# Twelve output-weight blocks instead of eight ahead of the last V tile, and their products behind it

## The chip, the core and the metric

The kernel runs on one core of one Trainium2 chip. The metric is the device time of one execution in microseconds (us). The kernel before was run three times: 680.56, 680.35 and 680.41 us, median 680.41. One further execution was profiled; every row of the trace quoted here is from that execution.

## What is computed

One decode step of grouped-query attention over a cache, gated by a small MLP. All data are float32.

```python
# x (8, 512); k_cache, v_cache (8, 8, 4096, 128); wq (512, 4096); wo (4096, 512)
xn = layernorm(x)
q  = heads(xn @ wq)                         # 8 batches, 32 heads of 128, 4 per cache head
p  = softmax(q . k_cache * 128 ** -0.5)     # over 4096 cached keys
o  = p . v_cache                            # (8, 32 heads, 128)
s  = o.reshape(8, 4096) @ wo                # (8, 512)
g  = silu(mlp(xn))                          # gelu, layernorm, scale, output projection
out = x + s * g
```

The caches are 268 MB of the 291 MB that are read, so the kernel is a stream of large loads with the arithmetic laid beside it.

## The kernel before

**Stages.** wq and the MLP's weights are loaded, q is projected and the MLP's gate worked out (L347 to L349). Then the loop of L350 goes over eight cache heads h. Each head takes two K tiles (`scores`, L269), a `softmax` (L272 to L298), and two V tiles (`values`, L310), one per half of the eight batches. A tile is 128 partitions x 64 KB, 8 MB, and goes into one of three buffers named `slot` (L67, L75). A load can start when the instructions that read the buffer's tile of three loads ago are done.

**Values and combine.** `values` multiplies one group of batches by V into one of two accumulators `o_ps`; VectorE then picks the diagonal (L313) and sums it (L315) into `o_sb`; `combine` (L320) folds `o_sb` into `po` by one small matmul, which is called one group late, so that TensorE has the next group to do meanwhile. The last V tile of the last head is loaded as two halves of 4 MB and is handled as two groups (n = 2); each group is 16 matmuls, and each shows as two records in the trace, 32 a group.

**Output weights.** wo is 32 blocks m of 128 x 512, 256 KB each; block m belongs to head m // 4 of the cache and its query row r = m % 4. All 32 share one slot buffer, loaded on the same queue (SyncE, SP) as everything else. The kernel before loads blocks 0 to 7 (`WO_EARLY = 8`, L359), then the last V tile's two halves (L332), then blocks 8 to 31 in nine pieces (`WO_PIECES`, L362) of 6, 5, 4, 3, 2, 1, 1, 1 and 1 blocks. Every load on the queue takes one of eight completion semaphores in turn, so it is not issued until the load eight before it has landed.

**Products of wo.** `project_o` (L344) multiplies blocks 0 to 27, whose heads are done early, into `part`, the first half of `sc`; the blocks r = 0 to 3 of a head go to four different 32-column strips of TensorE's array. Blocks 26 and 27 are cut in two halves of 256 columns each, to all four strips. `part` is then copied to SBUF (L383) and folded into the accumulator `acc` (L399). Blocks 28 to 31 belong to the last head; `direct` multiplies them straight into `acc` (L391) once `combine` has delivered that head: 28 and 29 ahead of L399, 30 and 31 behind it. VectorE multiplies `acc` by the gate, adds x (L403, L404), and the result is stored (L405).

**Order.** Each engine does its instructions in the order of its queue; a scheduler (Tile) makes the queues from the program's order and the dependences. In the kernel before, TensorE's queue around the end is: 32 matmuls of the first V tile of the last head; products 0 to 7; combine; 16 matmuls of the last tile's first half; combine; 16 matmuls of its second half; products 8 to 12; combine; products 13 to 27; direct 28, 29; L399; direct 30, 31.

Of the kernel before, what the change touches and what calls it, by code (L numbers as in the profile page):

```python
# [15 lines left out]
HKV, REP, S, DH = 8, 4, 4096, 128  # L16
NK = D // P
G = 4
J = S // (G * P)
R = 32  # L20
# [9 lines left out]
HALF = B // 2  # L30
# [1 line left out]
SLOT = HALF * UNIT  # L32
W = 64
OUT_ROWS = 2 * B
WO_EARLY = 8
WO_PIECES = [(8, 14), (14, 19), (19, 23), (23, 26), (26, 28), (28, 29), (29, 30), (30, 31), (31, 32)]
FOLDED = HKV * REP - REP
AHEAD = FOLDED + 2

# [20 lines left out]
def tile_gqa_gmlp_decode(ctx: ExitStack, tc: tile.TileContext, x, kT, v, wq, wo, w_mlp, w_ex0, w_ex1, w_ex2, w_ex3, out, gate, stored):  # L60
    nc = tc.nc
# [12 lines left out]
    def slot():  # L74
        return ring.tile([P, SLOT], F32, name="slot")  # L75
# [188 lines left out]
    def scores(h, half, k_sb):  # L264
        for i in range(HALF):
            b = half * HALF + i
            for c in range(2):
                for g in range(G):
                    nc.tensor.matmul(sc[R * g:R * (g + 1), c, :], qz[:, h, b * R:(b + 1) * R],  # L269
                                     k_sb[:, i, c, g, :], start=(b == 0), stop=(b == B - 1))  # L270

    def softmax(h):  # L272
        m = nm[:, h:h + 1]
        nc.vector.tensor_reduce(m, sc, op=ALU.max, axis=AX.XY, negate=True)  # L274
        p = work.tile([P, J * P], F32, name="p")
        nc.scalar.activation(p, sc.rearrange("p c s -> p (c s)"), AF.Exp,  # L276
                             bias=m, accum_out=l[:, h:h + 1])
        a = scratch([1, P], "a")
        nc.tensor.transpose(a, m, ident)  # L279
        nmin = small.tile([1, R], F32, name="nmin")  # L280
        nc.vector.tensor_reduce(nmin, a.rearrange("b (g r) -> b r g", g=G), op=ALU.min, axis=AX.X)
        full = small.tile([1, G, R], F32, name="full")
        nc.vector.tensor_copy(full, nmin[:, None, :].to_broadcast([1, G, R]))  # L283
        mm = scratch([P, 1], "mm")
        nc.tensor.transpose(mm, full.rearrange("b g r -> b (g r)"), ident[:1, :1])  # L285
        w = small.tile([P, 1], F32, name="w")
        nc.vector.tensor_sub(w, mm, m)
        nc.scalar.activation(w, w, AF.Exp)
        wl = small.tile([P, 1], F32, name="wl")
        nc.vector.tensor_mul(wl, w, l[:, h:h + 1])  # L290
        tot = scratch([P, 1], "tot")
        nc.tensor.matmul(tot, same_all, wl, start=True, stop=True)  # L292
        nc.vector.reciprocal(wl, tot)
        nc.vector.tensor_scalar(p, p, w, wl, op0=ALU.mult, op1=ALU.mult)  # L294
        pT = work.tile([P, J, B, G, REP], F32, name="pT")
        nc.vector.transpose(pT.rearrange("p j b g r -> p j g b r"),  # L296
                            p.rearrange("p (j g b r) -> p j g b r", j=J, g=G, b=B))
        return pT.rearrange("p j b g r -> p j b (g r)")  # L298
# [3 lines left out]
    def values(b0, n, pT, v_sb):  # L302
        o = o_ps[turn[0] % 2]
        turn[0] += 1
        of = o.rearrange("p g d -> p (g d)")
        rows = HALF // n
        for j in range(J):
            for i in range(n):
                c = i * rows + j % rows
                nc.tensor.matmul(of[R * c:R * c + G * REP, :], pT[:, j, b0 + i],  # L310
                                 v_sb[:, i, j], start=(j < rows), stop=(j >= J - rows))
        o_all = work.tile([P, G, DH], F32, name="o_all")
        nc.vector.tensor_mul(o_all, o, diag[:, :, None].to_broadcast([P, G, DH]))  # L313
        o_sb = small.tile([P, DH], F32, name="o_sb")
        nc.vector.tensor_reduce(o_sb, o_all.rearrange("p g d -> p d g"), op=ALU.add, axis=AX.X)  # L315
        return b0, n, o_sb

    def combine(b0, n, o_sb, po):
        f = fold if n == HALF else fold_last
        nc.tensor.matmul(po[:, b0 * REP:(b0 + n) * REP], o_sb, f.rearrange("p i r -> p (i r)"),  # L320
                         start=True, stop=True)

    def load_k(h, half):
        t = slot()
        nc.sync.dma_start(t, kT[h, half])
        return t.rearrange("p (i c g s) -> p i c g s", i=HALF, c=2, g=G)

    def load_v(h, half, parts):
        t = slot()
        n = SLOT // parts  # L330
        for c in range(parts):
            nc.sync.dma_start(t[:, c * n:(c + 1) * n], v[h, half][:, c * n:(c + 1) * n])  # L332
        return t.rearrange("p (i j e) -> p i j e", i=HALF, j=J)
# [3 lines left out]
    def project_o(lo, hi):  # L337
        for m in range(lo, hi):
            h, r = divmod(m, REP)
            cuts = 2 if m >= FOLDED - 2 else 1  # L340
            n = D // cuts
            for i in range(cuts):
                q = 2 * (r % 2) + i if cuts == 2 else r
                nc.tensor.matmul(part[R * q:R * q + B, i * n:(i + 1) * n], oT[:, h, r, :],  # L344
                                 wo_sb[:, m, i * n:(i + 1) * n], start=(m < REP), stop=(cuts == 2))
# [4 lines left out]
    for h in range(HKV):  # L350
        for half in range(2):
            scores(h, half, load_k(h, half))
        pT = softmax(h)
        po = po_ps[:, h % 2]
        for half in range(2):
            last = h == HKV - 1 and half == 1
            if last:
                wo_slot = slot()
                nc.sync.dma_start(wo_slot[:, :WO_EARLY * D], wo[:, :WO_EARLY * D])  # L359
                v_sb = load_v(h, half, 2)  # L360
                for lo, hi in WO_PIECES:
                    nc.sync.dma_start(wo_slot[:, lo * D:hi * D], wo[:, lo * D:hi * D])  # L362
                wo_sb = wo_slot.rearrange("p (m d) -> p m d", d=D)
                project_o(0, WO_EARLY)
            else:
                v_sb = load_v(h, half, 1)
            n = 2 if last else HALF
            for i in range(0, HALF, n):
                done = values(half * HALF + i, n, pT, v_sb[:, i:i + n])
                if half or i:  # L370
                    combine(*o_prev, po)
                o_prev = done
        combine(*o_prev, po)
        po_t = po.rearrange("p (b r) -> p r b", r=REP)
        if h < HKV - 1:
            nc.vector.tensor_copy(oT[:, h], po_t)
        else:
            for a in range(2):
                nc.vector.tensor_copy(oT_last[:, :, a, a * B:(a + 1) * B], po_t)

    project_o(WO_EARLY, FOLDED)
    part_sb = work.tile([P, G, DH], F32, name="o_all")
# [13 lines left out]
    for a in range(2):  # L396
        for g in range(G):
            c = (2 * g + a) * W
# [56 lines left out]
```

## Time and profile before

| | |
|---|---|
| median of three runs | 680.41 us (680.35 to 680.56) |
| the profiled execution | 680.28 us, of which the trace's span is 678.8 us |
| TensorE (PE) busy | 344.0 us, 51% of the span |
| VectorE (DVE) busy | 83.4 us, 12% |
| DMA | 290.80 MB read from HBM, 428 GB/s over the span |
| chain of work that ended last | DMA 79%, PE 16%, issue 4% |

Times in a view are us from the span's start. PE rows are matmuls, PEld rows weight loads, SPq rows the moments at which SyncE issues a transfer; the number behind the "x" is a count of records, and what stands in brackets is the idle time ahead of the first one and what ended it. A float32 matmul of 128 x 512 leaves two records. Matmuls are pipelined, so the time from the start of one to the start of the next tells what it costs, and the duration of one record is longer than that. A clock of 1.00 in a window is TensorE at full speed, 0.50 at half.

### The profile page before, as it was taken

The page shows a single profiled execution, that of the slowest core. Times are in us where ns is not written, and L with a number is a line of the kernel's source. Part 1 is how long each engine was busy: PE and PEld are TensorE (multiplying, and loading weights), DVE is VectorE, ACT ScalarE, POOL GpSimd, SP SyncE. Part 2 cuts the span into 40 slices and gives each one's busy share as a digit, 9 for nine tenths or more (in the row PEclk, how much of TensorE's full clock was granted, in tenths as well). Part 3 has the DMA queues.
Part 4 walks back from the last instruction along what each step waited for, and adds up shares of the span by engine and source line. Part 5 has one row for each costly group of instructions (what it writes and reads, how often), then busy time and mean ns, then how long its engine had stood idle before and what let it go on. Part 6 is the DMA issues. An engine that isn't in the chain of part 4 may idle for free.

```text
span 678.8 us, 5218 instructions
## 1 busy us (share of the span) xinstructions
PE 344.0 (51%) x2415; PEld 92.5 (14%) x2415; DVE 83.4 (12%) x159; ACT 13.4 (2%) x27; POOL 7.9 (1%) x17
## 2 busy tenths in 40 slices
PE   0448744446655454555554344555544345555567
PEld 0112211111111011111111011111111011111111
DVE  1143021102110021101100021101101021100221
ACT  0010000000000000000000000000000000000000
POOL 3000000000000000000000000000000000000000
PEclk9987866787776568777666778877666787876679
DMA  9999999999999999999999999999999999999997
GB/s 386 453 441 430 430 433 430 433 430 433 434 433 430 433 433 430 433 441 440 434 433 430 436 436 434 440 434 433 430 433 430 433 433 434 430 436 433 419 427 315
DMA packets 6741, 291.16 MB, mean 429 GB/s; under 512 B 888, under 2 KB 888, under 8 KB 1688
## 3 DMA queue, kind: packets, MB, share of 16 engines
q1 hardware_dynamic: 6576, 290.80, 99.1%
q8 instruction: 19, 0.31, 0.2%
q10 hardware_dynamic: 144, 0.03, 0.0%
q14 instruction: 2, 0.02, 0.0%
HBM read 290.80 MB, written 0.03 MB: 428 GB/s over the span
## 4 chain that ended last, share of the span: by engine, by line
DMA 79%; PE 16%; issue 4%; DVE 0%; SPq 0%; POOLq 0%; POOL 0%
DMA slot<-in_kT 36%; DMA slot<-in_v 33%; PE sc L269 7%; PE o_ps L310 7%; DMA slot<-in_wo 7%; DMA slot<-in_x 3%; PE scr L224 1%; PE scr L228 1%; SPq L332 0%; PE scr L217 0%; DVE st L146 0%; POOLq L449 0%; POOL rstd L149 0%; PE scr L206 0%; PE acc L391 0%
## 5 line engine op out<-in xcount | busy, mean ns | idle before, releaser
L269 PE MATMUL sc<-slot,qz 128*32 128x512 f32 x1024 | 145.4, 731 | 131.2 <-DMA slot<-in_kT 131.2
L310 PE MATMUL o_ps<-slot,pT 128*16 128x512 f32 x1024 | 148.2, 743 | 110.0 <-DMA slot<-in_v 110.0
L269 PEld LDWEIGHTS sc<-slot,qz 128*32 128x32 f32 x1024 | 38.1, 131 | 232.0 <-issue 149.4
L310 PEld LDWEIGHTS o_ps<-slot,pT 128*16 128x16 f32 x1024 | 32.9, 114 | 211.0 <-issue 151.5
L274 DVE TENSOR_REDUCE nm<-sc 128x1 f32<-128x1024 f32 x8 | 9.8, 1225 | 273.7 <-PE sc L269 273.7
L313 DVE TENSOR_TENSOR o_all<-o_ps,diag 128x512 f32<-128x512 f32 x17 | 11.8, 692 | 244.8 <-PE o_ps L310 244.8
L276 ACT ACTIVATE p<-sc,nm 128x1024 f32<-128x1024 f32 x8 | 8.9, 1114 | 551.8 <-DVE nm L274 551.8
L320 PE MATMUL po_ps<-fold,o_sb 128*128 128x16 f32 x30 | 6.0, 274 | 26.8 <-DVE o_sb L315 26.8
L315 DVE TENSOR_REDUCE o_sb<-o_all 128x128 f32<-128x512 f32 x17 | 17.8, 1047 | 0.6
L153 PE MATMUL scr<-ident,slot 8*128 8x8 f32 x4 | 0.6, 254 | 25.0 <-DVE slot L150 25.0
L320 PEld LDWEIGHTS po_ps<-fold,o_sb 128*128 128x128 f32 x30 | 4.5, 189 | 40.6 <-DVE o_sb L315 40.6
L296 DVE STREAM_TRANSPOSE pT<-p 128x1024 f32<-128x1024 f32 x8 | 10.0, 1246 | 0.3
L249 PE MATMUL scr<-slot,xnT 128*32 128x512 f32 x64 | 8.9, 708 | 0.3 <-issue 0.3
L344 PE MATMUL sc<-slot,oT 128*8 128x512 f32 (+1 forms) x60 | 8.4, 565 | 1.1 <-DMA slot<-in_wo 1.0
L279 PE MATMUL scr<-ident,nm 128*1 128x128 f32 x8 | 2.2, 270 | 10.8 <-DVE nm L274 10.8
L292 PE MATMUL scr<-wl,same 128*128 128x1 f32 x16 | 3.6, 297 | 6.5 <-DVE wl L290 6.5
L294 DVE TENSOR_SCALAR p<-p,w,wl 128x1024 f32<-128x1024 f32 x8 | 6.5, 813 | 0.3
L224 PE MATMUL scr<-slot,rest 128*32 128x512 f32 x10 | 5.4, 1044 | 0.0
L187 PE MATMUL scr<-part_sum,same 128*128 128x1 f32 x4 | 1.1, 348 | 8.4 <-DVE part_sum L185 8.4
L285 PE MATMUL scr<-ident,full 1*128 1x1 f32 x8 | 1.8, 220 | 5.0 <-DVE full L283 5.0
L292 PEld LDWEIGHTS scr<-wl,same 128*128 128x128 f32 x16 | 3.2, 249 | 7.0 <-PE scr L285 7.0
L153 PEld LDWEIGHTS scr<-ident,slot 8*128 8x128 f32 x4 | 0.5, 208 | 25.0 <-DVE slot L150 25.0
(94 smaller groups left out, 69.0 us busy)
## 6 DMA issues: line engine op xcount, KB each, us to landing
slot<-in_v SPq DMA_DIRECT2D x2, 4096.0 KB, 28.7
slot<-in_w_mlp SPq DMA_DIRECT2D x1, 4928.0 KB, 32.7
slot<-in_wo SPq DMA_DIRECT2D x1, 2048.0 KB
slot<-in_wo SPq DMA_DIRECT2D x1, 1536.0 KB
slot<-in_wo SPq DMA_DIRECT2D x1, 1280.0 KB, 37.9
slot<-in_wo SPq DMA_DIRECT2D x1, 1024.0 KB
slot<-in_wo SPq DMA_DIRECT2D x4, 256.0 KB, 18.7
slot<-in_wo SPq DMA_DIRECT2D x1, 768.0 KB
```

The source lines that it names most:

```text
L224: nc.tensor.matmul(pw[R * g:R * (g + 1), :], hT[:, a, R * g:R * (g + 1)], w_out_sb[:, i, :], start=(a == 0), stop=False)
L249: nc.tensor.matmul(pq[R * g:R * (g + 1), :], xnT[:, k, :], wq_sb[:, k, lo:lo + REP * DH], start=(k == 0), stop=(k == NK - 1))
L269: nc.tensor.matmul(sc[R * g:R * (g + 1), c, :], qz[:, h, b * R:(b + 1) * R], k_sb[:, i, c, g, :], start=(b == 0), stop=(b == B - 1))
L274: nc.vector.tensor_reduce(m, sc, op=ALU.max, axis=AX.XY, negate=True)
L276: nc.scalar.activation(p, sc.rearrange("p c s -> p (c s)"), AF.Exp, bias=m, accum_out=l[:, h:h + 1])
L292: nc.tensor.matmul(tot, same_all, wl, start=True, stop=True)
L296: nc.vector.transpose(pT.rearrange("p j b g r -> p j g b r"), p.rearrange("p (j g b r) -> p j g b r", j=J, g=G, b=B))
L310: nc.tensor.matmul(of[R * c:R * c + G * REP, :], pT[:, j, b0 + i], v_sb[:, i, j], start=(j < rows), stop=(j >= J - rows))
L313: nc.vector.tensor_mul(o_all, o, diag[:, :, None].to_broadcast([P, G, DH]))
L315: nc.vector.tensor_reduce(o_sb, o_all.rearrange("p g d -> p d g"), op=ALU.add, axis=AX.X)
L320: nc.tensor.matmul(po[:, b0 * REP:(b0 + n) * REP], o_sb, f.rearrange("p i r -> p (i r)"), start=True, stop=True)
L344: nc.tensor.matmul(part[R * q:R * q + B, i * n:(i + 1) * n], oT[:, h, r, :], wo_sb[:, m, i * n:(i + 1) * n], start=(m < REP), stop=(cuts = ...
```

## The change

Twelve blocks instead of eight are loaded ahead of the last V tile. Their products are no longer put in the program ahead of that tile's first matmul; `values` now hands back its last matmul, and the twelve products are issued after the last matmul of the tile's second half (`tc.issue_after`). The other twenty blocks come in seven pieces of 7, 5, 4, 1, 1, 1 and 1 blocks instead of twenty-four in nine.

```diff
-WO_EARLY = 8
-WO_PIECES = [(8, 14), (14, 19), (19, 23), (23, 26), (26, 28), (28, 29), (29, 30), (30, 31), (31, 32)]
+WO_EARLY = 12
+WO_PIECES = [(12, 19), (19, 24), (24, 28), (28, 29), (29, 30), (30, 31), (31, 32)]
...
-                nc.tensor.matmul(of[R * c:R * c + G * REP, :], pT[:, j, b0 + i],
+                mm = nc.tensor.matmul(of[R * c:R * c + G * REP, :], pT[:, j, b0 + i],
                                  v_sb[:, i, j], start=(j < rows), stop=(j >= J - rows))
...
-        return b0, n, o_sb
+        return (b0, n, o_sb), mm
...
                 wo_sb = wo_slot.rearrange("p (m d) -> p m d", d=D)
-                project_o(0, WO_EARLY)
...
-                done = values(half * HALF + i, n, pT, v_sb[:, i:i + n])
+                done, mm = values(half * HALF + i, n, pT, v_sb[:, i:i + n])
                 if half or i:
                     combine(*o_prev, po)
+                if last and i + n == HALF:
+                    with tc.issue_after(mm.ins):
+                        project_o(0, WO_EARLY)
```

As built, TensorE's queue around the end becomes: 32 matmuls of the first V tile of the last head; combine; 16 matmuls of the last tile's first half; combine; 16 of its second half; products 0 to 11; combine; products 12 to 27; direct 28, 29; L399; direct 30, 31. The queues of the other compute engines have the same instructions in the same order. On SP two issues are gone. Of the last pieces, block 29's now waits for the landing of the last head's first V tile, block 30's for that of blocks 0 to 11, and block 31's for that of the last V tile's first half; in the kernel before, five pieces wait so, the last one (block 31) for the piece of blocks 8 to 13. The lines behind the edit stand two further down in the changed kernel (L391 becomes L393).

## The prediction

> **What bounds the kernel now.** I read the page's chain first, then its last pieces in order of time (start us, us, what), then the queues around the end.
>
> ```profile
> span 678.8 us, 5218 instructions
> DMA 79%; PE 16%; issue 4%; DVE 0%; SPq 0%; POOLq 0%; POOL 0%
> ...
> 629.35 35.71 DMA slot<-in_wo
> 665.06 0.02 issue
> 665.08 11.13 DMA slot<-in_wo
> 676.21 0.04 issue
> 676.25 0.46 PE acc L391 x16
> 676.71 0.02 issue
> 676.74 0.24 DVE gate L403
> ```
>
> The load stream bounds it to the last: the last wo piece lands at 676.21, and behind it stand 16 records of block 31 (0.46), two VectorE operations and the store. The span ends 678.8 − 676.74 = 2.06 after L403 starts. What counts is how far TensorE is behind the stream there. Its rows from the last V tile on, with VectorE's copy of `part`:
>
> ```profile
> 651.74 6.39 PE L310 MATMUL o_ps<-slot,pT 128*16 128x512 f32 x32 [3.60 <-DMA slot<-in_v]
> 660.04 0.39 PE L320 MATMUL po_ps<-fold_last,o_sb 128*128 128x8 f32 x2 [1.91 <-DVE o_sb L315]
> 661.45 4.96 PE L310 MATMUL o_ps<-slot,pT 128*16 128x512 f32 x32 [1.02 <-DMA slot<-in_v]
> 666.23 1.88 PE L344 MATMUL sc<-slot,oT 128*8 128x512 f32 x10
> 668.32 0.39 PE L320 MATMUL po_ps<-fold_last,o_sb 128*128 128x8 f32 x2 [0.21 <-DVE o_sb L315]
> 668.64 2.99 PE L344 MATMUL sc<-slot,oT 128*8 128x512 f32 x20
> 672.43 1.04 PE L344 MATMUL sc<-slot,oT 128*8 128x512 f32 x6 [0.81 <-DMA slot<-in_wo]
> 673.71 0.62 PE L344 MATMUL sc<-slot,oT 128*8 128x256 f32 x8 [0.24 <-DMA slot<-in_wo]
> 674.40 0.69 DVE L383 COPY o_all<-sc 128x512 f32<-128x512 f32 x1 [5.36 <-PE sc L344]
> 675.20 0.41 PE L399 MATMUL acc<-o_all,pick 128*16 128x64 f32 x16
> 675.61 0.42 PE L391 MATMUL acc<-slot,oT_last 128*16 128x64 f32 x16
> 676.25 0.42 PE L391 MATMUL acc<-slot,oT_last 128*16 128x64 f32 x16 [0.22 <-DMA slot<-in_wo]
> ```
>
> The tile's halves land at 651.74 and 661.45 (each start was released by in_v). Three waits for in_wo, 0.81, 0.24 and 0.22 us, show that TensorE is just ahead of the stream, with slack of a us or two, not ten.
>
> **The change part by part.** *The stream.* The same 32 blocks are loaded, four of them now ahead of the tile. Its first half took until 651.74, its second until 661.45: 9.71 us for 4 MB, so four blocks (1 MB) cost 2.43. The halves land at 654.17 and 663.88; blocks 12 on land as before, since the bytes ahead of them are the same. Do the two pieces less save anything? SP's rows:
>
> ```profile
> 651.71 0.33 SPq L362 DMA_DIRECT2D slot<-in_wo  x1
> 661.42 0.33 SPq L362 DMA_DIRECT2D slot<-in_wo  x1
> 665.08 0.33 SPq L362 DMA_DIRECT2D slot<-in_wo  x1
> ```
>
> The second half landed at 661.42 and the next piece, six blocks, at 665.08 (the load that waits for it was issued then): 0.61 a block. The last two single blocks were taken at 675.61 and 676.25, 0.64 apart. So a small piece costs some 0.03 more, and two pieces less save 0.06; ends 0 and 0.2, taken 0.1. It is hidden if TensorE ends last. The issues come early: block 31's went out at 665.08, 11 us ahead of its landing, and would now wait only for the first half (654.2).
>
> *TensorE behind the tile.* Its queue then holds the second half's 16 matmuls, 12 products, combine, 14 products, the four cut ones, direct 28 and 29, L399, direct 30 and 31. Before, 5 and 13 whole products stood there; the eight others ran between V tiles, while TensorE waited. The pitch is read from the weight loads:
>
> ```profile
> 663.13 0.17 PEld L310 LDWEIGHTS o_ps<-slot,pT 128*16 128x16 f32 x4 [0.68 <-issue]
> 663.98 0.17 PEld L310 LDWEIGHTS o_ps<-slot,pT 128*16 128x16 f32 x4 [0.68 <-issue]
> 664.52 0.11 PEld L310 LDWEIGHTS o_ps<-slot,pT 128*16 128x16 f32 x4 [0.37 <-issue]
> 664.95 0.11 PEld L310 LDWEIGHTS o_ps<-slot,pT 128*16 128x16 f32 x4 [0.32 <-issue]
> ...
> 666.24 0.10 PEld L344 LDWEIGHTS sc<-slot,oT 128*8 128x8 f32 x4 [0.33 <-issue]
> 666.66 0.09 PEld L344 LDWEIGHTS sc<-slot,oT 128*8 128x8 f32 x1 [0.33 <-issue]
> 667.09 0.09 PEld L344 LDWEIGHTS sc<-slot,oT 128*8 128x8 f32 x1 [0.34 <-issue]
> ```
>
> Four records go together (four column strips), 0.85 us apart until 664, then 0.43. Five products are records 4, 4, 1, 1: up to four products with different strips take two pitches, and so does one left over. At the short pitch: a half tile 8 x 0.43 = 3.43 (8 of 0.429); 12 products, three fours, 2.57; 14, four groups, 3.43. Combine took 668.32 to 668.64, 0.32; there it waited for VectorE, which the 2.57 now cover (the 660.04 row came 1.91 us after its tile's end). [...]
>
> So, with L for what the clock takes from the second half, the cut products start at 663.88 + 3.43 + L + 2.57 + 0.32 + 3.43 = 673.63 + L. From there to L403: copy starts 674.40 − 673.71 = 0.69 later and takes 0.69; 675.20 − 675.09 = 0.11 to L399; then L399 and direct 30. L399 to direct 30 was 0.41 with part of it a wait for its block; a batch of 16 costs between 0.2 (half of that) and 0.41, two of them 0.4 to 0.8. Last, 676.74 − 676.25 = 0.49. Sum 2.38 to 2.78. L403 starts at 676.01 + L to 676.41 + L, plus 0 to 0.3 for combine. I take 676.2 + L, near the low ends, since batches overlap: the shift against 676.74 is **L − 0.55**, from L − 0.73 to L − 0.03. Blocks 24 to 27 land by 663.88 + 16 x 0.61 = 673.6 and 31 at 676.2, so no load is late.
>
> *L, the clock.* Windows of 3.41 us, cut so that the granted clock has one value in each (664.18 is where the pitch changed); columns: us; busy us (records) of PE, PEld, DVE, ACT, POOL; granted clock; DMA share; GB/s.
>
> ```profile
> 647.12:650.53 3.41, 0.82 (x6) 0.30 (x2) 0.57 (x1) 0.00 (x0) 0.00 (x0) 1.00 1.05 452
> 650.53:653.94 3.41, 2.20 (x12) 0.49 (x16) 0.00 (x0) 0.00 (x0) 0.00 (x0) 0.50 1.07 461
> 653.94:657.36 3.42, 3.42 (x20) 0.68 (x16) 0.00 (x0) 0.00 (x0) 0.00 (x0) 0.50 0.96 406
> 657.36:660.77 3.41, 1.16 (x10) 0.30 (x2) 1.74 (x2) 0.00 (x0) 0.00 (x0) 1.00 0.88 376
> 660.77:664.18 3.41, 2.73 (x16) 0.66 (x20) 0.00 (x0) 0.00 (x0) 0.00 (x0) 0.50 1.01 430
> 664.18:667.60 3.42, 3.42 (x34) 0.70 (x22) 1.08 (x2) 0.00 (x0) 0.00 (x0) 1.00 0.99 418
> 671.01:674.43 3.42, 2.28 (x22) 0.25 (x15) 0.03 (x1) 0.00 (x0) 0.00 (x0) 1.00 0.86 339
> ```
>
> The clock is 1.00 or 0.50 for a whole window, by the one before: from half, 2.20 us busy did not raise it, 2.73 did; from full, 1.16 lost it, 2.28 kept it. Half speed costs half the time spent in it. Before, 661.45 to 664.18 was at half: L = 1.37 (661.45 + 3.43 + 1.37 = 666.25; the row says 666.23). With the tile at 663.88 it begins just ahead of a boundary: unless the window 660.77 to 664.18 is 2.7 us busy, 664.18 to 667.60 is at half and L is 1.71 to 1.86, by whether the last 0.3 ahead of it is at full. With the boundaries elsewhere, d after the landing: d over 2.7 (a fifth of positions) gives L = d/2, 1.35 to 1.71; d under 2.7 gives (d + 3.41)/2, 1.71 to 3.05, but 1.71 where the first half's work (3.43 + half-speed loss, from 654.17) holds the clock up to d, which by the 1.16 and 2.28 bounds can be so for d to about 1.2. Half of the positions give under, half over, about 1.95.
>
> [...]
>
> So the forecast: L 1.95, shift 1.4. The profiled execution, 680.28 us, is 0.13 under the median of 680.41; the shift is added to the median: **681.8 us**.
>
> **The rivals.** (1) *The clock is already full when the second half lands, and the stream still ends last.* From L under 0.55 TensorE is ready before block 31, and the time is that of the stream, 680.41 − 0.1 = 680.3: not slower. For it: the halves stay 9.7 us apart, and the first half's work is dense to some 660. Against it: 657.36 to 660.77, with 1.16 us busy, lost the clock, and between the halves only combine (0.39) runs.
>
> [...]
>
> (2) *One more window at half speed.* If the first full window of the second half falls short of what raises the clock, the twelve products run at half too: another 3.41/2 = 1.7 on the largest L, 4.75 − 0.55, a shift of 4.2, 684.6. All windows shown from 2.73 up were followed by full.
>
> (3) *Fewer loads shorten the stream itself,* each load having a price of its own. For it the 0.64 against 0.61; if TensorE kept up too, twice the upper price 0.1 gives 680.2, and no more than rival 1.
>
> [...]
>
> (4) *The twelve products don't move:* excluded by the built queue; if they ran ahead of the tile after all, shift L − 0.55 − 2.57, below zero, 680.3.
>
> **How the numbers follow.** Forecast 0.80; rival 1 0.10; rival 2 0.05; rivals 3 and 4 0.02; 0.03 for a gain that I see no cause for. I count 0.2%, 1.36 us, as what a measurement of this kernel can tell from no change. The forecast's shift is over 1.36 where L is over 1.91, a little over half of the positions, and the constants are open more upward (to L − 0.03) than downward: 0.63 of it. Slower 0.80 x 0.63 + 0.05 = 0.55; faster 0.03, the last case; same 0.42, with rivals 1, 3 and 4. The forecast's own range is 1.35 − 0.73 to 3.05 − 0.55, 681.0 to 682.9. Rival 1 pulls the low end down by some, the upper bound of combine the high end up by 0.1: 680.6 to 683.0.
>
> **What would show it.** In the changed profile: L310's last two groups start 2.4 later (654.2, 663.9); the first L344 row follows its tile without a wait, 24 records in about 2.6 us; no L344 or L393 row waits for in_wo; the chain's last stretch is PE from the second half's landing, not DMA; L403 starts 0.6 to 2.6 later with the clock row of the window behind 663.9 at 0.50. I am wrong if the last L393 batch waits for in_wo (rival 1), if the halves land less than 2 us later, or if the first products run at a pitch of 0.85 (rival 2).

## The result, and the profile after

Over 22 executions of each kernel the median goes from 680.45 to 681.79 us, +1.34; the ratio is 1.0021 (95% interval 1.0015 to 1.0027). The kernel before stays within 680.27 to 680.77; the changed one spreads from 680.67 to 683.32. The profiled execution of the changed kernel took 681.79 us, with a span of 680.5.

The chain of waits of the changed kernel, its last pieces (start us, us, what):

```profile
628.07 35.76 DMA slot<-in_v
663.82 0.04 issue
663.87 5.32 PE o_ps L310 x32
669.19 2.58 PE sc L344 x24
671.77 0.32 PE po_ps L320 x2
672.09 4.03 PE sc L344 x28
676.11 0.02 issue
676.14 0.70 DVE o_all L385
676.84 0.04 issue
676.88 0.42 PE acc L401 x16
677.30 0.49 PE acc L393 x32
677.79 0.02 issue
677.81 0.24 DVE gate L405
```

Before, the chain was loads down to block 31 at 676.21. Now the last load in it is the V tile's second half, and behind it TensorE works through without one wait for wo: the half, the twelve products (2.58), combine (0.32), the rest (4.03), the copy of `part`, and the last small batches. L405 starts at 677.81; its counterpart L403 stood at 676.74. The engine's own rows in order of time show the landings and the missing waits:

```profile
654.21 5.21 PE L310 MATMUL o_ps<-slot,pT 128*16 128x512 f32 x32 [6.02 <-DMA slot<-in_v]
...
663.87 5.32 PE L310 MATMUL o_ps<-slot,pT 128*16 128x512 f32 x32 [2.15 <-DMA slot<-in_v]
669.01 2.76 PE L344 MATMUL sc<-slot,oT 128*8 128x512 f32 x24
671.70 0.39 PE L320 MATMUL po_ps<-fold_last,o_sb 128*128 128x8 f32 x2
672.01 3.82 PE L344 MATMUL sc<-slot,oT 128*8 128x512 f32 x34
```

The halves start 2.47 and 2.42 us later than before (651.74, 661.45). L, the clock's part of the second half, is 669.01 − 663.87 − 3.43 = 1.71. The clock by windows of the changed kernel, cut where the granted clock changed (columns as in the prediction):

```profile
654.03:657.45 3.42, 3.24 (x16) 0.66 (x20) 0.00 (x0) 0.00 (x0) 0.00 (x0) 0.50 1.06 460
657.45:660.86 3.41, 1.97 (x20) 0.32 (x12) 1.33 (x2) 0.00 (x0) 0.00 (x0) 1.00 0.84 363
660.86:664.27 3.41, 0.79 (x6) 0.43 (x10) 0.41 (x1) 0.00 (x0) 0.00 (x0) 1.00 0.97 416
664.27:667.69 3.42, 3.42 (x20) 0.77 (x16) 0.00 (x0) 0.00 (x0) 0.00 (x0) 0.50 1.00 426
667.69:671.10 3.41, 3.41 (x36) 0.90 (x32) 1.78 (x2) 0.00 (x0) 0.00 (x0) 1.00 1.00 415
```

A window with 1.97 us of TensorE's work kept the clock full and the next, with 0.79, lost it. So 0.40 us behind its start the second half fell to half speed for a whole window of 3.41 us, which cost 1.71.

L405 starts 1.07 us later than L403 did; the span is 1.7 longer. The rest is behind L405, and the transfers of the last microseconds show it. First the changed kernel from 677 to 681 us, then the kernel before over its whole run (issue, KB, us to landing):

```profile
q10 hardware_dynamic: 144, 0.03, 4.5%
q8 instruction: 1, 0.02, 2.1%
...
out<-gate ACTq DMA_DIRECT2D x1, 32.0 KB, 2.1
```

```profile
out<-gate ACTq DMA_DIRECT2D x1, 32.0 KB, 1.5
```

The output store takes 0.6 us more. By the packets' times, the one packet on the instruction queue (q8), a block of 16 KB, was fetched from 678.00 to 679.32, and the store's packets ran from 679.20 to 679.71. In the kernel before the fetch ran from 676.43 to 677.60, and the store's first packet came at 678.12. The prediction had no such term.

### The profile page after: what moved, and what is told of

Same layout as the page of the kernel before. It is cut to its first block, busy times and chain, and to the rows that moved or that the text cites. A ratio compares the mean times of both kernels' runs of the same rounds, so it can differ in the third digit from the quotient of the medians.

```text
span 680.5 us, 5216 instructions
## 1 busy us (share of the span) xinstructions
PE 339.0 (50%) x2415; PEld 92.0 (14%) x2415; DVE 83.4 (12%) x159; ACT 13.4 (2%) x27; POOL 7.9 (1%) x17
## 4 chain that ended last, share of the span: by engine, by line
DMA 77%; PE 18%; issue 4%; DVE 1%; SPq 0%; POOLq 0%; POOL 0%
DMA slot<-in_v 38%; DMA slot<-in_kT 35%; PE o_ps L310 8%; PE sc L269 7%; DMA slot<-in_x 3%; PE sc L344 1%; PE scr L224 1%; PE scr L228 1%; PE scr L217 0%; DVE o_all L385 0%; DVE st L146 0%; POOLq L451 0%; POOL rstd L149 0%; PE acc L393 0%; PE scr L206 0%
## 5 line engine op out<-in xcount | busy, mean ns | idle before, releaser
L269 PE MATMUL sc<-slot,qz 128*32 128x512 f32 x1024 | 142.6, 719 | 132.4 <-DMA slot<-in_kT 132.4
L344 PE MATMUL sc<-slot,oT 128*8 128x512 f32 (+1 forms) x60 | 6.8, 564 | 0.0
```

## Experiments

All times are medians; where a run was timed, the kernel before was run with it (680.41 to 680.48). The end is measured from the second half's first matmul to the first gate operation (L403 before, L405 and others in the edited kernels), which leaves out small shifts of the whole stream.

### Loads and products apart

`e1_ahead`: the loads as changed, the products ahead of the tile again.

```diff
+                project_o(0, WO_EARLY)
             else:
...
-                if last and i + n == HALF:
-                    with tc.issue_after(mm.ins):
-                        project_o(0, WO_EARLY)
```

> Twelve blocks and seven pieces as in the changed kernel, but the twelve products stand ahead of the last V tile, as the eight did before. Theory A (TensorE's queue behind the last half sets the end: halves 2.43 us late, and 2.57 us of products behind them): behind the half stand 5 and 9 products, so L403 could start at 663.88 + 3.43 + L + 2.09 (combine waits for VectorE, 668.32 - 666.23 in the kernel before) + 0.32 + 2.57 + 2.57 = 674.9 + L, and the stream (676.6) ends last while L is under 1.8: median 680.3 to 680.8, scatter upward to 681.9. Rival B (the late halves alone make the loss, wherever the products stand): about 681.8, as the changed kernel.

681.09 us (680.85 to 681.29; ratio 1.0009, 1.0001 to 1.0018): above theory A's median, below B's 681.8, and nearly without scatter. Its profile's L was 1.71 too, but the clock no longer set the end:

```profile
664.11 5.32 PE L310 MATMUL o_ps<-slot,pT 128*16 128x512 f32 x32 [2.19 <-DMA slot<-in_v]
669.25 1.88 PE L344 MATMUL sc<-slot,oT 128*8 128x512 f32 x10
...
673.85 1.25 PE L344 MATMUL sc<-slot,oT 128*8 128x512 f32 x10 [0.30 <-DMA slot<-in_wo]
...
677.07 0.23 DVE L403 TENSOR_TENSOR gate<-acc,gate 128x64 f32<-128x64 f32 x1 [0.99 <-PE acc L391]
out<-gate ACTq DMA_DIRECT2D x1, 32.0 KB, 2.1
```

TensorE waits for the piece of blocks 24 to 27 (673.85). Two whole products then run ahead of the cut ones and of the copy; before, only the cut ones were in that piece. L403 comes 677.07 − 664.11 = 12.96 behind the half, where the changed queue with the same L took 13.94. And the store again takes 2.1.

`e2_eight_behind`: eight blocks and nine pieces as before, the eight products behind the tile.

```diff
-WO_EARLY = 12
-WO_PIECES = [(12, 19), (19, 24), (24, 28), (28, 29), (29, 30), (30, 31), (31, 32)]
+WO_EARLY = 8
+WO_PIECES = [(8, 14), (14, 19), (19, 23), (23, 26), (26, 28), (28, 29), (29, 30), (30, 31), (31, 32)]
```

> Eight blocks and nine pieces as before, but the eight products queued behind the last V tile. Theory A: the half lands at 661.45; 661.45 + 3.43 + L + 2.09 + 0.32 + 4.29 (18 products, five groups) + 2.57 = 674.1 + L, under the stream's 676.7 while L is under 2.6: median 680.4 to 680.6, at most 681.3 in one execution. Rival C (queueing the products behind the tile alone makes the loss): 681.4 or more in the median.

680.50 us (680.29 to 681.18; ratio 1.0003, 0.9994 to 1.0011), as theory A had it; two of eleven executions were near 681.1. So the products behind the tile without the late halves give 0.1. The late halves with the new pieces, but without the products, give 0.7, half of the loss, though by the piece and the store and, in the profile, not by the clock. Both together give 1.34.

### More of the same, and the clock

`e3_sixteen`: sixteen blocks ahead, products behind.

```diff
-WO_EARLY = 12
-WO_PIECES = [(12, 19), (19, 24), (24, 28), (28, 29), (29, 30), (30, 31), (31, 32)]
+WO_EARLY = 16
+WO_PIECES = [(16, 21), (21, 25), (25, 28), (28, 29), (29, 30), (30, 31), (31, 32)]
```

> The same change taken further: sixteen blocks ahead, their products behind, seven pieces for the other sixteen. Theory A: 26 whole products behind the half as in the changed kernel (seven groups of four either way), but the half lands another 2.43 us later: 681.8 + 2.4 = 684.2, first half at 656.6, second at 666.3. Rival (the loss is one late window of the clock, not the landing): 681.8 again.

684.68 us (682.28 to 685.77, six executions): 2.9 above the changed kernel where theory A had 2.4. The halves started at 656.78 and 666.44, 2.57 later each; L405 came 13.75 behind the second with L = 1.53. The price of an early load goes on once TensorE's slack is used up.

`e4_warm`: the changed kernel, with 16 added matmuls between the halves.

```diff
                 v_sb = load_v(h, half, 1)
+                v_warm = v_sb
...
+                if last and i + n < HALF:
+                    with tc.issue_after(mm.ins):
+                        t = scratch([P, 512], "warm")
+                        for w in range(16):
+                            c = R * (w % 4)
+                            nc.tensor.matmul(t[c:c + G * REP, :], pT[:, w // 4, half * HALF + w % 4],
+                                             v_warm[:, w % 4, w // 4], start=True, stop=True)
```

> The changed kernel with 16 matmuls of 16 x 512 more between the tile's halves, on the first V tile of the last head, into a scratch bank that nobody reads; they keep TensorE busy until about 663 and change no output. Theory A with L as the clock's part: the second half begins at full clock, L is 0 to 0.6 (a late end of the added matmuls included), and the time falls to the stream's 680.3 to 680.6 with little scatter. Rival D (the clock is not the cause, the 2.43 us and the products are): no gain, 681.8; if the added matmuls hold the queue up, 682 and more.

680.57 us (680.43 to 681.00). More work on TensorE, 1.2 us less time. Its rows:

```profile
659.24 3.61 PE L377 MATMUL scr<-slot,pT 128*16 128x512 f32 x32
662.78 0.39 PE L320 MATMUL po_ps<-fold_last,o_sb 128*128 128x8 f32 x2
664.18 3.63 PE L310 MATMUL o_ps<-slot,pT 128*16 128x512 f32 x32 [1.01 <-DMA slot<-in_v]
...
673.96 1.25 PE L344 MATMUL sc<-slot,oT 128*8 128x512 f32 x10 [0.57 <-DMA slot<-in_wo]
...
677.18 0.23 DVE L413 TENSOR_TENSOR gate<-acc,gate 128x64 f32<-128x64 f32 x1 [0.99 <-PE acc L401]
out<-gate ACTq DMA_DIRECT2D x1, 32.0 KB, 1.5
```

The half takes 3.63 us instead of 5.32 and L is 0. The piece of blocks 24 to 27 sets the end, 13.00 behind the half as in `e1_ahead`: a floor. But the store is back at 1.5 too, so this run alone doesn't tell the clock from the store. `e1_ahead` and `e4_warm` have the same floor and stores of 2.1 and 1.5, and their medians are 0.52 apart: the store's part. `e4_warm` and `e8_shift` (below) both have a store of 1.5, and their medians, 680.57 and 681.40, are 0.8 apart: the clock's part.

`r1_again` and `r2_again`: the changed kernel, profiled twice more.

> The changed kernel unchanged, profiled once more. If the windows of the clock run freely, the half-speed stretch lies elsewhere and L (first product's start minus the half's start minus 3.43) is another than 1.71; L405 starts 12.23 + L behind the half's first matmul (as it did in the changed profile, 13.94 with L 1.71), but not before about 677.1, where the piece of blocks 24 to 27 lets it. The output store takes 1.9 to 2.1 us to land.

> As the run before it: another L, and L405 at 12.23 + L behind the half's first matmul. If the clock's windows stood still against the kernel's start, L would be 1.71 again in both.

681.53 and 682.87 us. The second's rows:

```profile
664.04 6.54 PE L310 MATMUL o_ps<-slot,pT 128*16 128x512 f32 x32 [1.12 <-DMA slot<-in_v]
670.41 2.75 PE L344 MATMUL sc<-slot,oT 128*8 128x512 f32 x24
...
679.20 0.23 DVE L405 TENSOR_TENSOR gate<-acc,gate 128x64 f32<-128x64 f32 x1 [0.99 <-PE acc L393]
out<-gate ACTq DMA_DIRECT2D x1, 32.0 KB, 1.8
```

L is 670.41 − 664.04 − 3.43 = 2.94, and L405 comes 15.16 behind the half: 12.22 + L. `r1_again` had L 1.71 and 13.95, `e3_sixteen` 1.53 and 13.75, `e8_shift` 1.37 and 13.59. So the time behind the half is 12.2 + L, with an L that differs between executions of one kernel. The windows (two of `r1_again`, then one of `r2_again`) show why:

```profile
658.09:661.50 3.41, 1.67 (x16) 0.22 (x8) 1.63 (x2) 0.00 (x0) 0.00 (x0) 1.00 1.05 453
661.50:664.92 3.42, 1.37 (x14) 0.65 (x18) 0.11 (x1) 0.00 (x0) 0.00 (x0) 1.00 0.90 387
663.13:666.55 3.42, 2.51 (x12) 0.49 (x16) 0.00 (x0) 0.00 (x0) 0.00 (x0) 0.50 0.99 423
```

The boundary behind the landing comes after 0.40 us in the changed kernel's first profile, 0.98 in `r1_again` and 2.51 in `r2_again`. `r1_again` missed its expectation of another L: its half-speed window lies elsewhere, but again wholly inside the second half, which gives 1.71. In `r2_again` the half began at half speed, and 2.51 us of work did not raise the clock at the boundary, so the next window ran at half speed too (a granted clock of 0.56 on average over 666.92 to 670.34). L makes most of the scatter of the changed kernel, and the store, with 1.8 to 2.1, the rest that the profiles show.

### The store and the fetch

`e8_shift`: the changed kernel with 16 matmuls added in the sixth head's stage.

```diff
+                if h == 5 and not half:
+                    t = scratch([P, 512], "extra")
+                    for w in range(16):
+                        c = R * (w % 4)
+                        nc.tensor.matmul(t[c:c + G * REP, :], pT[:, w // 4, w % 4],
+                                         v_sb[:, w % 4, w // 4], start=True, stop=True)
```

> The changed kernel with 16 matmuls of 16 x 512 more in the sixth head's stage, where TensorE waits for loads, into a scratch bank that nobody reads; they change no output and nothing of the end but the place at which TensorE's last block of instructions is fetched. Theory E (in the changed kernel's profile the last 16 KB of instructions are fetched at 678.0 to 679.3, on one of the DMA engines of the output store at 679.2, whose landing comes 2.1 us after its issue instead of 1.5): the fetch moves some 1.5 us ahead of the store, the store takes 1.5 again, and the median falls by 0.4 to 0.65, to 681.1 to 681.4, with L403 to L405 starting no earlier. Rival (the store's 0.6 us has another cause): 681.8, store 2.1.

681.40 us (680.43 to 682.65; ratio 1.0013, 1.0005 to 1.0022), 0.39 under the changed kernel, at the edge of what was expected; the two kernels' intervals overlap, so the size is not sure. In the profile the fetch moved to 675.6 to 676.8, and the store is back at 1.5 (L405's counterpart, then the store):

```profile
677.63 0.23 DVE L411 TENSOR_TENSOR gate<-acc,gate 128x64 f32<-128x64 f32 x1 [0.99 <-PE acc L399]
...
out<-gate ACTq DMA_DIRECT2D x1, 32.0 KB, 1.5
```

Over all thirteen profiles, read by the packets' times: where the fetch's packet ended 0.5 us or more ahead of the store's first packet, the store landed 1.5 us after its issue (seven profiles); where it ended less than 0.3 ahead or ran into the store, 1.8 to 2.1 (six). In all six the landing came 0.6 to 0.7 us behind the store's last packet, against 0.35 in the seven. In four of them some of the store's packets also took longer, up to 155 ns instead of 18, but in `r1_again` and `r2_again`, where the fetch had ended 0.3 us before, none did. So the store's time goes with the fetch's place, and moving the fetch brought the 1.5 back; how the fetch delays the landing stays open. In the changed kernel's first profile nine of the store's 144 packets, a sixteenth, took 33 to 155 ns where the others took 18 at most, and the first of the nine started at 679.32, where the fetch ended. That the fetch and these nine were on one DMA engine is an estimate from these numbers, since no view shows a packet's engine.

### Pieces, and a version without the three terms

`e5_pieces`: the kernel before with twelve pieces instead of nine.

```diff
-WO_PIECES = [(8, 14), (14, 19), (19, 23), (23, 26), (26, 28), (28, 29), (29, 30), (30, 31), (31, 32)]
+WO_PIECES = [(8, 11), (11, 14), (14, 16), (16, 19), (19, 21), (21, 23), (23, 26), (26, 28), (28, 29), (29, 30), (30, 31), (31, 32)]
```

> The kernel before with its 24 blocks in twelve pieces instead of nine (the first three pieces cut in two). By the prediction's step that a piece costs 0.03 to 0.1 us of the stream: 680.5 to 680.75. [...]

680.56 us, 0.11 more, within its interval (0.9993 to 1.0011). In the profiles block 31's batch started 24.51 us behind the first half before (676.25 − 651.74) and 24.64 here (676.75 − 652.11): 0.04 a piece, where the prediction had 0.03.

`e7_between`: the twelve products behind the tile's first half.

```diff
-                if last and i + n == HALF:
+                if last and i + n < HALF:
```

> The changed kernel, its twelve products queued behind the tile's first half instead of its second. Theory A and F: behind the second half stand 5 and 9 products, so TensorE is ready in time, but the piece of blocks 24 to 27 and the store's meeting with the fetch stay: 680.9 to 681.2, like the kernel with the products ahead, not 681.8. Rival (any queueing behind the tile's matmuls costs the 1.3 us): 681.8.

680.61 us (680.53 to 681.14), below the expected range: a miss of 0.3. L405 came 12.98 behind the half, the floor of the piece; the store took 1.9 in the profile, and the five highest executions, 680.90 to 681.14, stand apart from the six at 680.53 to 680.61, by about the store's price; so the store seems to meet the fetch in some executions only.

`e9_recut`: products ahead, pieces cut at 20, 26 and 28, and the added matmuls of `e8_shift`.

```diff
-WO_PIECES = [(12, 19), (19, 24), (24, 28), (28, 29), (29, 30), (30, 31), (31, 32)]
+WO_PIECES = [(12, 20), (20, 26), (26, 28), (28, 29), (29, 30), (30, 31), (31, 32)]
...
+                project_o(0, WO_EARLY)
...
-                if last and i + n == HALF:
-                    with tc.issue_after(mm.ins):
-                        project_o(0, WO_EARLY)
+                if h == 5 and not half:
...
```

> Twelve blocks ahead of the tile, their products ahead of it too, the other twenty in seven pieces cut at 20, 26 and 28 instead of 19, 24 and 28, and the 16 added matmuls in the sixth head's stage. Theory F (with the products ahead, the 0.65 us by which that kernel stood over the one before were 0.35 from the piece of blocks 24 to 27, whose two whole products run between its landing and the cut ones, and the rest from the store meeting the fetch): both go, and the stream with two loads less sets the end: 680.3 to 680.5, no slower than the kernel before. Rival (the half tile that lands 2.43 us late costs it by itself): 681 as with the old cut.

680.76 us, and mostly in two groups: four executions at 680.29 to 680.32, five at 680.93 to 681.27. A miss for F as stated. The profile, of the upper group, has a store of 1.5 and L = 2.56 (the half at 664.20, the first product at 670.19), and with such an L even 5 and 9 products behind the half end after the stream: the gate's first operation comes 13.31 behind the half. The clock's term has to go too.

`e10_best`: products between the halves, pieces cut at 17, 22, 26 and 28, and the added matmuls.

```diff
-WO_PIECES = [(12, 19), (19, 24), (24, 28), (28, 29), (29, 30), (30, 31), (31, 32)]
+WO_PIECES = [(12, 17), (17, 22), (22, 26), (26, 28), (28, 29), (29, 30), (30, 31), (31, 32)]
...
-                if last and i + n == HALF:
+                if last and i + n < HALF:
...
+                if h == 5 and not half:
...
```

> Twelve blocks ahead, their products between the last tile's halves, so that the clock is full for the second; the other twenty in eight pieces cut at 17, 22, 26 and 28, so that only the cut blocks are in the piece ahead of the single ones; and the 16 added matmuls in the sixth head's stage, which keep the fetch of instructions off the store. All three terms gone: the stream sets the end in every execution, 680.3 to 680.45 with little scatter, store 1.5, L403 released by in_wo; the kernel before is 680.45. If one of the terms was named wrongly, 680.6 or more stays.

680.37 us (680.27 to 680.55; the kernel before 680.48 beside it; ratio 0.9998, 0.9989 to 1.0007): the loss is gone, and no gain over the kernel before can be told. Its rows:

```profile
663.96 3.63 PE L310 MATMUL o_ps<-slot,pT 128*16 128x512 f32 x32 [0.71 <-DMA slot<-in_v]
...
676.27 0.42 PE L399 MATMUL acc<-slot,oT_last 128*16 128x64 f32 x16 [0.21 <-DMA slot<-in_wo]
...
676.76 0.23 DVE L411 TENSOR_TENSOR gate<-acc,gate 128x64 f32<-128x64 f32 x1 [1.67 <-PE acc L399]
```

L is 0, and block 31's batch waits for in_wo again: the stream ends last, 12.80 behind the half, so that the piece's floor of 13.0 was worth 0.2, not the 0.35 expected of it above.

## Why the prediction was right, and where it was lucky

**The landing.** Halves at 654.17 and 663.88 were predicted; 654.21 and 663.87 came.

**The queue behind the half.** The sum put L403 at 676.2 + L, 12.32 + L behind the half; five profiles show 12.22 + L (three of the changed kernel, one with sixteen blocks and `e8_shift`), within 0.02. The low ends were right to take: L401 and the two batches behind it took 0.93 to L405 (676.88 to 677.81), where the sum had 0.89 to 1.29. No run shows what the sum's 0 to 0.3 for combine stood for: by the rows combine began 2.69 behind the first product (669.01 to 671.70), where 2.57 was taken, and took 0.31 (to 672.01), where 0.32 was taken, so 0.11 in all. The chain turned from loads to TensorE as forecast, and the twelve products took 2.58 in it.

**The clock.** Half speed cost half its time: a whole window of 3.41 us at 0.50 cost 1.71. The working of L from d, the time from the landing to the next boundary, held too: d of 0.40, 0.98 and 2.51 in the three profiles of the changed kernel gives 1.71, 1.71 and 2.96, and 1.71, 1.71 and 2.94 came; `e8_shift` (d 2.75, L 1.37) and `e3_sixteen` (3.08, 1.53) fit too. That the boundaries can lie anywhere, on which the middle of L rests, no run had shown when the forecast was made. The three profiles of the changed kernel have them in three places, so they move between executions; that all places are equally likely is not shown. 0.79 and 1.37 us of work in 3.41 lost the clock, as 1.16 did before.

The middle of L was taken too high: 1.95, where the two executions profiled nearest to the median have 1.71. Counting the store's 0.3 to 0.6, the median's 1.34 leaves 0.7 to 1.0 for TensorE. Against a stream that ends some 12.86 behind the half (15.29 − 2.43 from the kernel before), that is an L of about 1.4 to 1.7 in the middle, an estimate. A likely cause, not tried: 1.67 us of work held the clock and 1.37 lost it, where the rows before bounded this only between 1.16 and 2.28, so the first half's work would hold the clock in more positions than was taken. The bound is not one of busy time alone: in the kernel before, 1.89 us of work in matmuls of 64 columns (674.43 to 677.84) lost the clock.

**What was missed.** "From there to L403" and on, the end behind L403 was taken as the same 2.06 us. It grew to 2.7 (680.5 − 677.81), since the store met the fetch of instructions. The two errors, L too large by some 0.3 to 0.6 and a store too short by 0.3 to 0.6, cancelled. That the forecast of 681.8 met the median of 681.79 is luck; the mechanism is not.

**"So no load is late."** True for the forecast, where TensorE is later still. It is wrong for rival 1: behind the landing of blocks 24 to 27 come two whole products besides the cut ones, which with the clock full sets a floor of 13.0, so that `e4_warm` stood at 680.57, not at 680.3.

**The rivals.** Rival 1 was excluded as the usual course by the chain of waits; its mechanism was produced by `e4_warm` and `e10_best`. It may still happen now and then: 680.67 and 680.77 of the changed kernel's 22 executions, and 680.43 and 680.52 of `e8_shift`'s eleven, lie under 681.0, the low end of the forecast's own range. None of these was profiled. Rival 2 (products at half pitch) did not show: the twelve took 2.58 in each profile of the changed kernel, even behind an L of 2.94; the slowest execution, 683.32, was not profiled. Rival 3's price is 0.04 a load by the traces. Rival 4 was excluded by the order of the rows.

## What to carry to other kernels

A stream that is busy to its end hides the engine behind it only up to that engine's slack; loads moved ahead of the tile that it waits for spent the slack twice here, as a later landing (2.42 us) and as more work queued behind it (2.58). Where the slack was gone, a time that had agreed within 0.5 us scattered over 2.65 us, mostly by the clock's windows (L of 1.71 to 2.94 in three profiles), so judge such a change by many executions and by the distance from the last landing. If there is other work for the engine, put it into the gap ahead of the late tile, where it also kept the clock full here (the second half took 3.63 us instead of 5.32 in `e4_warm`, `e7_between` and `e10_best`).

## What was not expected of the hardware

Instructions come by DMA too: the page of the changed kernel lists a queue of the kind "instruction" (q8) with 19 packets, 0.31 MB, 16 KB each. Where the last block's fetch ended less than 0.3 us ahead of the output store's first packet, or later, the store landed 0.3 to 0.6 us later; 16 matmuls added on TensorE in the sixth head's stage moved the fetch from 678.00 to 675.6, out of the way. That the last block holds TensorE's instructions is inferred from this move. Added instructions made the kernel faster in `e4_warm`, by 1.2 us; in `e8_shift` the 0.39 is not clear of the scatter.
